# Two pairs of squared scores in one buffer, and one DMA transpose of 2048 columns in place of two of 1024

## The chip, the core and the metric

The kernel runs on one core of a Trainium2 chip. The metric is the device time of one execution in microseconds; lower is better. Shown for the kernel before are three runs: 765.41, 765.5 and 766.83 us, median 765.5 us. A profile is one further execution, taken by the hardware profiler. In it PE is TensorE (matmuls), PEld its loading of weights, DVE is VectorE, ACT is ScalarE, POOL is GpSimd, and SP is SyncE, whose queue issues nearly all DMAs of this kernel in program order.

## The reference

Two stages follow each other, for 8 batches of 3200 positions and 256 features.

```python
# first stage: z is 8 x 3200 x 64, u and v are 8 x 3200 x 256
scores = (1.0 / S) * np.matmul(z, z.transpose(0, 2, 1))
attn = np.maximum(scores, 0.0) ** 2
x = u * np.matmul(attn, v)
# second stage: w_q, w_k are 256 x 64, w_out is 256 x 256
W_tok = (1.0 / np.sqrt(dh)) * np.einsum('bsd,btd->bst', x @ w_q, x @ w_k)
mixed = np.einsum('bst,btd->bsd', W_tok, x)
out = np.maximum(mixed, 0.0) @ w_out
```

The score matrix of a batch is symmetric, since both of its factors are z. Only the first stage needs it element by element; in the second, `(x w_q)((x w_k)^T x)` is reassociated, so that a 64 x 256 matrix stands between.

## The kernel before

**Tiles of scores.** A batch's 3200 columns are split into seven groups: six of 512 columns and a last one of 128 (`LASTG`). The 3200 rows are 25 row tiles of 128. A *tile* in the list `tiles` (L253 to L281) is one row tile of scores for one group, 128 x 512; for the last group four row tiles of 128 columns make one. Tiles are handled in pairs: `scores(p0)` (L296) has TensorE fill two PSUM banks, one tile in each, `first_stage` (L316) has DVE or ACT take the positive part into an SBUF tile `g` (float32), and `second_stage` (L326) has ACT or POOL square `g` into an SBUF tile `at` of 2 x 512 columns in float16. `at` then serves as the stationary operand of the product with v (`second_product`, L464), which adds over all 25 row tiles into the accumulators `acc`.

**Turned tiles.** Since the scores are symmetric, a tile of group gi whose rows lie in a later group gj is, transposed, a tile of group gj. `is_turned(gi, gj)` (L237) says for which pairs of groups this is used: gj up to two further than gi, and (0, 4), never with the last group. That makes ten pairs of groups a batch, of four row tiles each. Their squares are turned by a DMA transpose from `at` into a tile `tt` (L342 to L352), one `tt` for each pair of groups, and when group gj is computed, the rows in question are not scored again but read from `tt`; these rows are the list `left` of the main loop (L1106). Row tile 24 of groups 3, 4 and 5 is turned likewise into small tiles `ts` for the last group. The seven `tt` buffers are planned at L285 to L293.

**Order of the tiles.** For each group the loop at L254 lists the turned row tiles (`near`) and the others (`own`) in twos, interleaved evenly, so that both tiles of a turned pair are neighbours and lie in one `at`; `odd` puts a tile ahead where a group starts at an odd place in the list. In `second_stage`, two neighbouring turned tiles become one transpose of 1024 columns (L340), a lone one a transpose of 512. The first group of the first batch has the order in which z arrives (`ZCH`).

**Buffers.** The pool `pat` hands out `NAT` = 11 buffers of one pair each, in turn (L50, L63). A buffer is filled again once TensorE has read all of it and its transposes have landed. The first four of them hold z, cast to float16, at the start (`zd`, L117 to L121), which TensorE turns at L130.

**The main loop.** One iteration (L1028 to L1231) scores up to three pairs (n = 6 tiles), takes the first stage of these, squares the pairs scored in the iteration before (`waiting`, L1080 to L1095), and has TensorE add up the tiles scored two iterations before (`LAG` = 2, L1099), a share of `left` with them (L1123). The order of instructions on every engine is that of the program, as written out by this loop and by the two scripts `OPENING` and `ENDING`. On SP's queue the transposes of `at` take their turn with those of x (L518), of the keys (L551) and of z (L176), with the loads of u (L195) and of v and z (L147), and with the stores of the output (L740). When a group closes, `gate` (L488) multiplies by u. Projections, keys, mixing and output of earlier groups are laid between the products.

**TensorE in two lanes.** Most matmuls contract over 64 of the 128 rows, and two of them run side by side in the two halves of the array (`first_pass`, `second_pass`, L401 to L418): each half of an `at` tile is read in one pass and the other half in the other.

```python
        ready = made_by[k - LAG]
...
        rows_ = [t for _, _, tis in tiles[consumed : consumed + new] for t in tis]
        old = len(left) if closes else min(len(left), max(0, size - len(rows_)))
        rows_ += left[:old]
        left = left[old:]
```

Of the kernel before, what the change touches and what calls it, by code (L numbers as in the profile page):

```python
# [9 lines left out]
FP16 = mybir.dt.float16  # L10
# [6 lines left out]
def kernel(  # L17
# [10 lines left out]
    nc = tc.nc  # L28

    B, S, D = u.shape  # L30
    dqk = z.shape[2]
    dh = moe_w_q.shape[1]
    P = 128
    NT = S // P
    ND = D // P
    W = 512
    widths = [512] * 6 + [128]
    starts = [sum(widths[:i]) for i in range(len(widths))]
# [8 lines left out]
    ALPHA = C1 * float(S) * float(S)  # L47
    FINAL_SCALE = 1.0 / (8.0 * ALPHA * ALPHA * ALPHA)

    NAT = 11  # L50

    consts = ctx.enter_context(tc.tile_pool(name="consts", bufs=1))
    pz = ctx.enter_context(tc.tile_pool(name="pz", bufs=1))
# [8 lines left out]
    pfo = ctx.enter_context(tc.tile_pool(name="pfo", bufs=2))  # L62
    pat = ctx.enter_context(tc.tile_pool(name="pat", bufs=NAT))  # L63
    ptt = ctx.enter_context(tc.tile_pool(name="ptt", bufs=1))
# [39 lines left out]
    zd0 = {}  # L104
# [12 lines left out]
    def cast_first(c, half, by):  # L117
        n0, nn = ZCH[c]
        if half == 0:
            zd0[c] = pat.tile([P, nn, 2, dqk], FP16, tag="at", name="zd")  # L120
        cast_by[by](out=zd0[c][:, :, half, :], in_=z32[n0][:])  # L121

    def turn_first(c):
# [111 lines left out]
    LASTG = NG - 1  # L235

    def is_turned(gi, gj):  # L237
        return gi < gj < LASTG and (gj <= gi + FAR or (gi, gj) == (0, 4))
# [5 lines left out]
    def group_of(ti):  # L244
        return max(gi for gi in range(NG) if starts[gi] <= ti * P)

    def rows_of(gi):
        return [starts[gi] // P + n for n in range(widths[gi] // P)]
# [4 lines left out]
    tiles, ends = [], {}  # L253
    for b in range(B):  # L254
        for gi in range(NG):
            near = [t for t in range(NT) if is_turned(gi, group_of(t))]
            own = [
                t for t in range(NT) if t not in near and not is_turned(group_of(t), gi)
            ]
            if gi == LASTG:  # L260
                own = [t for t in own if group_of(t) not in FOR_SMALL]
            if b == 0 and gi == 0:
                order = [t for n0, nn in ZCH for t in range(n0, n0 + nn)]
                assert sorted(order) == sorted(near + own)
            else:
                odd = len(tiles) % 2
                order, rest = own[:odd], own[odd:]
                n_, m_ = len(near) // 2, (len(rest) + 1) // 2
                at_ = sorted(
                    [((i + 0.5) / max(n_, 1), near[2 * i : 2 * i + 2]) for i in range(n_)]  # L270
                    + [((i + 0.7) / max(m_, 1), rest[2 * i : 2 * i + 2]) for i in range(m_)]
                )
                for _, two in at_:
                    order = order + two
                if rest and len(rest) % 2:
                    order.remove(rest[-1])
                    order.append(rest[-1])
            many = W // widths[gi]
            tiles += [(b, gi, order[i : i + many]) for i in range(0, len(order), many)]
            ends[b, gi] = len(tiles)  # L280
    NTILE = len(tiles)  # L281
# [4 lines left out]
    for b, gi, tis in tiles:  # L286
        gj = group_of(tis[0])
# [6 lines left out]
    made, turned = {}, {}  # L294
# [21 lines left out]
    def first_stage(p0, sc, on_act):  # L316
# [6 lines left out]
            )  # L323
        return g

    def second_stage(p0, g, on_act):  # L326
        at = pat.tile([P, 2 * W], FP16, tag="at", name="at")
        out = at[:].rearrange("p (a w) -> p a w", a=2)
        if on_act:
            nc.scalar.square(out=out, in_=g[:])  # L330
        else:
            nc.gpsimd.tensor_mul(out=out, in0=g[:], in1=g[:])  # L332
        blocks, turns = [], []
        for h, (b, gi, tis) in enumerate(tiles[p0 : p0 + 2]):
            for i, ti in enumerate(tis):
                made[b, gi, ti] = (at, h * W + i * widths[gi])
            gj = group_of(tis[0])
            if is_turned(gi, gj) or (gj == LASTG and gi in FOR_SMALL):
                blocks.append((b, gi, gj, tis[0] - starts[gj] // P, 1, h * W, (h + 1) * W))
        if len(blocks) == 2 and blocks[0][:3] == blocks[1][:3] and blocks[1][3] == blocks[0][3] + 1:  # L340
            blocks = [blocks[0][:4] + (2, blocks[0][5], blocks[1][6])]
        for b, gi, gj, n0, nn, c0, c1 in blocks:  # L342
            if gj == LASTG:
                turned[b, gi, gj] = ptt.tile([P, 1, 4, P], FP16, tag=f"ts{gi}", name=f"ts{gi}")
            elif (b, gi, gj) not in turned:
                home = tt_of[b, gi, gj]
                turned[b, gi, gj] = ptt.tile([P, 4, 4, P], FP16, tag=f"tt{home}", name=f"tt{home}")
            out = turned[b, gi, gj][:].rearrange("p n j t -> p (n j) t")
            turns.append(
                lambda out=out[:, 4 * n0 : 4 * (n0 + nn), :], c0=c0, c1=c1:  # L350
                nc.sync.dma_start_transpose(out=out, in_=at[:, c0:c1])
            )  # L352
        return turns

    accs = {}

# [44 lines left out]
    def first_pass(streams, banks, across):  # L401
        ends_ = {}

        def emit(lane, i, rows):
            ends_[lane] = i.emit(rows, i.start, False)

        for lane, rows in enumerate((LOW, HIGH)):
            for i in banks[lane ^ across]:
                streams.add(lane, width(i), lambda lane=lane, i=i, rows=rows: emit(lane, i, rows))
        return banks, across, max(streams.at), ends_  # L410
# [481 lines left out]
    now = [0]  # L892
# [74 lines left out]
    def shares(begins, closes, split, n):  # L967
        key = "s" if split else "b" if begins else "c" if closes else "m"
        key += "x" if mixing else "k" if keying else "p" if projecting else ""
        return shares_of[key][:n]  # L970
# [18 lines left out]
    def opening(order):  # L989
        sc, g = {}, {}  # L990
        for word in order.split():
            what, n, by = word[0], int(word[1:2]), word[2:]
            if what == "z":
                cast_first(n, int(by[0]), by[1])
            elif what == "t":
                turn_first(n)
            elif what == "c":
                place_first(n, by)
            elif what == "v":
                load_first_v(*[(0, 4), (12, 6), (18, 7), (4, 8)][n])  # L1000
            elif what == "s":
                sc[n] = scores(2 * n)
            elif what == "e":
                g[n] = first_stage(2 * n, sc.pop(n), by == "A")
            elif what == "q":
                each(second_stage(2 * n, g.pop(n), by == "A"))
            elif what == "w":
                warm(2 * int(word[1:]))
            elif what == "u":
                load_u(0, 0)  # L1010
            elif what == "m":
                ti = [t for x in tiles[2 * n : 2 * n + 2] for t in x[2]]
                for fn in whole(second_product(0, 0, ti, n == 0, False)):
                    fn()
        return [(2 * n, g[n]) for n in sorted(g)]
# [9 lines left out]
    left, first_sizes = [], [4, 5, 5, 5]  # L1025
    gate_pending = False
    ahead = []
    while groups:  # L1028
# [3 lines left out]
        n = 6  # L1032
# [7 lines left out]
        if mix_due(k):  # L1040
# [3 lines left out]
            n = 4  # L1044
        n = min(n, NTILE - produced)
# [45 lines left out]
        for i, x in enumerate([x for x in seconds if not x[2]]):  # L1091
            (late if i else soon).extend(second_stage(*x))
        for x in acts[:1]:
            each(second_stage(*x))
# [5 lines left out]
        b, gi = groups[0]  # L1100
        if begins:
# [4 lines left out]
            left = [t for t in range(NT) if t not in scored]  # L1106
        need = ends[b, gi]
        rest = len(left) + sum(len(tis) for _, _, tis in tiles[consumed:need])
# [7 lines left out]
        closes = steps == 1  # L1116
# [4 lines left out]
                new -= 1  # L1121
        rows_ = [t for _, _, tis in tiles[consumed : consumed + new] for t in tis]
        old = len(left) if closes else min(len(left), max(0, size - len(rows_)))  # L1123
        rows_ += left[:old]
        left = left[old:]
        consumed += new
# [10 lines left out]
        if on_lanes:  # L1137
# [7 lines left out]
            at_ = shares(begins, closes, split, len(between_))  # L1145
# [5 lines left out]
            if split:  # L1151
                cut = len(rows_) // 4
                if extra:
                    first = first_pass(streams, extra[0], across)
# [5 lines left out]
            elif extra and begins and uneven(extra):  # L1160
                first_extra = first_pass(streams, extra[0], across)
                first = first_pass(streams, banks, across)
# [3 lines left out]
            elif extra and begins:  # L1166
                first = first_pass(streams, extra[0], across)
                marks = [max(streams.at)]
                extra_second(first)
                first = first_pass(streams, banks, across)  # L1170
# [5 lines left out]
                at_ = [(x - 1) / total for x in marks + marks[1:]][: len(between_)]  # L1176
            elif extra:
                n_ = max(2, min(len(banks[0]) - 2, len(banks[0]) // 2))
                first = first_pass(streams, [bank[:n_] for bank in banks], across)
                first_extra = first_pass(streams, extra[0], across)  # L1180
                first = (banks, across) + first_pass(streams, [bank[n_:] for bank in banks], across)[2:]
# [35 lines left out]
        if closes:  # L1217
# [7 lines left out]
            left = None  # L1225
# [128 lines left out]
```

## Time and profile before

| | |
|---|---|
| median of three runs | 765.5 us (765.41 to 766.83) |
| span of the profiled execution, first to last instruction | 763.7 us |
| mean granted TensorE clock in it | 0.998 |
| bytes moved by DMA | 150.23 MB, mean 197 GB/s |
| DMA packets | 289614, of which 265168 under 512 B |
| read from HBM, written to HBM | 59.38 MB, 26.21 MB |

The profiled execution's own time is not given apart from its span; what lies around the span is taken as the difference to the median. In the tables of the profile a row names the line of the kernel, the engine, the operation and the tiles (out<-in), then the count. Busy times of an engine are unions over its instructions; the durations of matmuls are modelled at their ends. Duration triples are minimum, median and maximum in ns. "Landing" of a DMA is the time from the start of its issue to its completion. In a table of waits each row has who waited, for whom, us in total, number of times, longest.

### The profile page before, as it was taken

The numbers are of one execution on the slowest core, as the hardware profiler recorded it, in microseconds if no ns is written. First come the engines' busy times: TensorE is split into PE (matmuls) and PEld (weight loads), VectorE is DVE, ScalarE is ACT, GpSimd is POOL, SyncE is SP. The second block draws the span as 40 slices with busy tenths as digits, with TensorE's granted clock in tenths as the row PEclk, the third lists the DMA queues.
The fourth block names the chain that finished last, engine by engine and source line by source line (L and its number), as shares of the span: only waits on it lengthen the run. The fifth ranks groups of instructions, "written<-read, shape, count | busy, mean of one in ns | idle before, by whom it ended". The sixth has DMA issues, their size and how long they took to land.

```text
span 763.7 us, 29059 instructions
## 1 busy us (share of the span) xinstructions
PE 754.3 (99%) x12888; PEld 618.0 (81%) x12888; DVE 461.9 (60%) x458; ACT 551.1 (72%) x651; POOL 537.1 (70%) x351
## 2 busy tenths in 40 slices
PE   9999999999999999999999999999999999999996
PEld 6777888888888887888888888888878888888884
DVE  7655676546755567555665557656566565755534
ACT  8666776677767777687776877759777697776555
POOL 7897797768766678676787668866688665854540
PEclk9999999999999999999999999999999999999999
DMA  8999789887999969997899998999899999798636
GB/s 178 189 197 219 187 187 192 174 181 160 206 196 233 219 166 185 221 235 195 214 177 219 243 195 181 158 228 265 135 223 189 228 250 156 161 222 193 176 74 262
DMA packets 289614, 150.23 MB, mean 197 GB/s; under 512 B 265168, under 2 KB 268752, under 8 KB 289488
## 3 DMA queue, kind: packets, MB, share of 16 engines
q1 hardware_dynamic: 288768, 146.48, 91.2%
q0 software_dynamic: 576, 1.64, 1.1%
q8 instruction: 100, 1.64, 0.9%
q14 instruction: 26, 0.21, 0.1%
q10 hardware_dynamic: 144, 0.26, 0.1%
HBM read 59.38 MB, written 26.21 MB: 112 GB/s over the span
## 4 chain that ended last, share of the span: by engine, by line
PE 97%; DVE 2%; issue 0%; DMA 0%; ACT 0%; DVEq 0%; ACTq 0%
PE acc L369 72%; PE sc L307 12%; PE fo L369 5%; PE qk L369 5%; PE mx L657 1%; DVE x_sb L507 1%; DVE fo L1312 0%; DVE g L321 0%; PE ztp L130 0%; DMA z<-in_z_dram 0%; PE qk L610 0%; DVE zT L136 0%; PE xtx L634 0%; PE hd L644 0%; ACT fo L1316 0%
## 5 line engine op out<-in xcount | busy, mean ns | idle before, releaser
L321 DVE TENSOR_SCALAR g<-sc 128x1024 f32<-128x1024 f32 x329 | 400.5, 1223 | 240.5 <-PE sc L307 225.9
L332 POOL TENSOR_TENSOR at<-g 128x1024 f16<-128x1024 f32 x229 | 431.4, 1893 | 131.1 <-DVE g L321 106.5
L369 PE MATMUL acc<-v_sb,at 64*128 64x256 f16 (+1 forms) x7187 | 461.8, 269 | 1.6 <-DVE x_sb L507 0.5
L369 PEld LDWEIGHTS <-at 64*128 64x128 f16 (+1 forms) x7187 | 353.9, 94 | 86.9 <-PE acc L369 25.4
L330 ACT ACTIVATE at<-g 128x1024 f16<-128x1024 f32 x227 | 236.1, 1056 | 14.3 <-DVE g L321 7.2
L369 PE MATMUL acc<-v_sb,tt 64*128 64x256 f16 x2552 | 178.7, 269 | 0.0
L307 PE MATMUL sc<-zT 64*128 64x512 f16 (+1 forms) x1008 | 165.3, 357 | 0.2
L319 ACT ACTIVATE g<-sc 128x1024 f32<-128x1024 f32 x127 | 130.0, 1024 | 45.5 <-PE sc L307 43.2
L369 PEld LDWEIGHTS <-tt 64*128 64x128 f16 x2552 | 130.1, 94 | 14.2
L509 POOL TENSOR_TENSOR x_sb<-gt,u_sb 128x512 f16<-128x512 f32 x48 | 61.2, 1276 | 66.2 <-ACT gt L506 61.8
L678 ACT ACTIVATE rt<-mx 128x1024 f16<-128x1024 f32 x47 | 47.9, 1024 | 32.6 <-PE mx L657 32.5
L506 ACT COPY gt<-acc 128x512 f32<-128x512 f32 x48 | 28.0, 584 | 46.5 <-PE acc L369 44.7
L307 PEld LDWEIGHTS <-zT 64*128 64x128 f16 x1008 | 51.9, 94 | 8.8 <-issue 1.7
L369 PE MATMUL fo<-wo,rt 64*128 64x256 f16 (+1 forms) x696 | 57.9, 270 | 0.0
L544 ACT CAST qk<-qk 128x512 f16<-128x512 f32 x47 | 27.5, 585 | 34.3 <-PE qk L369 31.6
L369 PEld LDWEIGHTS <-rt 64*128 64x128 f16 (+1 forms) x696 | 35.5, 94 | 15.3 <-PE fo L369 6.3
L507 DVE TENSOR_TENSOR x_sb<-acc,u_sb 128x512 f16<-128x512 f32 x48 | 33.2, 691 | 20.3 <-PE acc L369 19.5
L739 ACT ACTIVATE fo<-fo 128x1024 f32<-128x1024 f32 x39 | 39.9, 1024 | 1.9 <-PE fo L369 1.7
L369 PEld LDWEIGHTS <-x_sb 64*128 64x128 f16 x672 | 29.8, 95 | 4.5 <-PE qk L369 0.9
L369 PE MATMUL qk<-kx,x_sb 64*128 64x64 f16 x672 | 32.8, 190 | 0.0
L369 PE MATMUL qk<-xT_sb,wkq 64*128 64x512 f16 (+3 forms) x118 | 25.8, 326 | 0.0
L369 PE MATMUL qk<-xT_sb,wqk 64*128 64x384 f16 (+3 forms) x148 | 24.8, 296 | 0.0
(86 smaller groups left out, 275.2 us busy)
## 6 DMA issues: line engine op xcount, KB each, us to landing
u_sb<-in_u_dram SPq DMA_DIRECT2D x48, 512.0 KB, 5.5
out_dram<-fo SPq DMA_DIRECT2D x43, 512.0 KB, 4.1
piece<-in_v_dram SPq DMA_DIRECT2D x42, 512.0 KB, 5.2
piece<-in_z_dram SPq DMA_DIRECT2D x7, 512.0 KB, 5.2
tt<-at SPq DMA_TRANSPOSE x162, 4.6
out_dram<-fo SPq DMA_DIRECT2D x9, 256.0 KB, 2.9
piece<-in_z_dram SPq DMA_DIRECT2D x7, 288.0 KB, 4.9
u_sb<-in_u_dram SPq DMA_DIRECT2D x8, 128.0 KB, 4.2
```

Source lines behind the costliest of these rows:

```text
L307: nc.tensor.matmul(out=sc[:, h, at : at + w], lhsT=zT[b][half : half + dqk, ds(z_at(b, h) + ti * P, P)], rhs=zT[b][half : half + dqk, ds(z ...
L319: nc.scalar.activation(out=g[:], in_=sc[:], func=RELU, scale=GSCALE)
L321: nc.vector.tensor_scalar(out=g[:], in0=sc[:], scalar1=0.0, scalar2=GSCALE, op0=AOP.max, op1=AOP.mult)
L330: nc.scalar.square(out=out, in_=g[:])
L332: nc.gpsimd.tensor_mul(out=out, in0=g[:], in1=g[:])
L369: return nc.tensor.matmul(out=self.out, lhsT=self.lhsT(rows), rhs=self.rhs(rows), start=start, stop=stop)
L506: nc.scalar.copy(out=upper[:], in_=accs[1][:])
L507: nc.vector.tensor_mul(out=x[:, 0:n], in0=accs[0][:, 0:n], in1=ug[:, 0:n])
L509: nc.gpsimd.tensor_mul(out=x[:, n : 2 * n], in0=upper[:], in1=ug[:, n : 2 * n])
L544: nc.scalar.copy(out=qks[b, gi][:, 0:gw], in_=out)
L678: nc.scalar.activation(out=out, in_=ps[:], func=RELU)
L739: nc.scalar.mul(out=flat_out[:, sl], in_=part, mul=FINAL_SCALE)
```

## The change

Five edits go together.

1. `pat` has 5 buffers of 2048 columns in place of 11 of 1024. Two pairs that follow each other in `tiles` (a *double*, numbered p0 // 4) share one: the pair that is squared first takes the buffer, the other one fills the second half.
2. The chunks of z at the start share buffers in twos.
3. The list of tiles puts turned and other row tiles in fours, with the start of a four at a multiple of 4 in the list.
4. The transposes of a double are issued after its second square has been emitted, and neighbouring turned tiles of one pair of groups go in one transpose, up to 2048 columns. Row tile 24 for the last group is still turned by itself, and at once.
5. In `left`, rows whose transposes have all been issued are moved to the front before a share is taken.

```diff
-    NAT = 11
+    NAT = 5
...
         if half == 0:
-            zd0[c] = pat.tile([P, nn, 2, dqk], FP16, tag="at", name="zd")
+            if c % 2 == 0:
+                zd0["both"] = pat.tile([P, 2, 8, 2, dqk], FP16, tag="at", name="zd")
+            zd0[c] = zd0["both"][:, c % 2, 0:nn, :, :]
...
-                odd = len(tiles) % 2
+                odd = -len(tiles) % 4
                 order, rest = own[:odd], own[odd:]
-                n_, m_ = len(near) // 2, (len(rest) + 1) // 2
+                n_, m_ = len(near) // 4, (len(rest) + 3) // 4
                 at_ = sorted(
-                    [((i + 0.5) / max(n_, 1), near[2 * i : 2 * i + 2]) for i in range(n_)]
-                    + [((i + 0.7) / max(m_, 1), rest[2 * i : 2 * i + 2]) for i in range(m_)]
+                    [((i + 0.5) / max(n_, 1), near[4 * i : 4 * i + 4]) for i in range(n_)]
+                    + [((i + 0.7) / max(m_, 1), rest[4 * i : 4 * i + 4]) for i in range(m_)]
                 )
...
+    doubles = {}
+
     def second_stage(p0, g, on_act):
-        at = pat.tile([P, 2 * W], FP16, tag="at", name="at")
-        out = at[:].rearrange("p (a w) -> p a w", a=2)
+        first = p0 // 4 not in doubles
+        if first:
+            doubles[p0 // 4] = pat.tile([P, 4 * W], FP16, tag="at", name="at"), []
+        at, parts = doubles[p0 // 4]
+        here = 2 * W * (p0 // 2 % 2)
+        out = at[:, here : here + 2 * W].rearrange("p (a w) -> p a w", a=2)
...
+                n0, c0 = tis[0] - starts[gj] // P, here + h * W
+                parts.append([b, gi, gj, n0, 1, c0, c0 + W])
+        blocks, turns = [], []
+        if first and p0 // 4 < (NTILE - 1) // 4:
+            now_, parts[:] = [x for x in parts if x[2] == LASTG], [x for x in parts if x[2] != LASTG]
+            parts = now_
+        else:
+            parts.sort(key=lambda x: x[5])
+        for part in parts:
+            was = blocks[-1] if blocks else None
+            if was and was[:3] == part[:3] and was[3] + was[4] == part[3] and was[6] == part[5]:
+                was[4] += 1
+                was[6] = part[6]
+            else:
+                blocks.append(part)
...
+    def turn_blocks(out, in_, key, tis):
+        for ti in tis:
+            turned_by[key + (ti,)] = now[0]
+        nc.sync.dma_start_transpose(out=out, in_=in_)
...
         old = len(left) if closes else min(len(left), max(0, size - len(rows_)))
+        if not closes:
+            left.sort(key=lambda t: not all((b, group_of(t), n) in turned_by for n in rows_of(gi)))
         rows_ += left[:old]
```

More of the change, by code (lines that the diff above doesn't have):

```diff
@@ L265 @@
             else:
-                odd = len(tiles) % 2
+                odd = -len(tiles) % 4
                 order, rest = own[:odd], own[odd:]
-                n_, m_ = len(near) // 2, (len(rest) + 1) // 2
+                n_, m_ = len(near) // 4, (len(rest) + 3) // 4
                 at_ = sorted(
-                    [((i + 0.5) / max(n_, 1), near[2 * i : 2 * i + 2]) for i in range(n_)]
-                    + [((i + 0.7) / max(m_, 1), rest[2 * i : 2 * i + 2]) for i in range(m_)]
-                )
[L273 to L277, printed above, removed]
+                    [((i + 0.5) / max(n_, 1), near[4 * i : 4 * i + 4]) for i in range(n_)]
+                    + [((i + 0.7) / max(m_, 1), rest[4 * i : 4 * i + 4]) for i in range(m_)]
+                )
+                for _, four in at_:
+                    order = order + four
+                short = rest[len(rest) // 4 * 4 :]
+                for t in short:
+                    order.remove(t)
+                order += short
             many = W // widths[gi]
@@ L332, in second_stage @@
             nc.gpsimd.tensor_mul(out=out, in0=g[:], in1=g[:])
-        blocks, turns = [], []
         for h, (b, gi, tis) in enumerate(tiles[p0 : p0 + 2]):
             for i, ti in enumerate(tis):
-                made[b, gi, ti] = (at, h * W + i * widths[gi])
+                made[b, gi, ti] = (at, here + h * W + i * widths[gi])
             gj = group_of(tis[0])
             if is_turned(gi, gj) or (gj == LASTG and gi in FOR_SMALL):
-                blocks.append((b, gi, gj, tis[0] - starts[gj] // P, 1, h * W, (h + 1) * W))
-        if len(blocks) == 2 and blocks[0][:3] == blocks[1][:3] and blocks[1][3] == blocks[0][3] + 1:
-            blocks = [blocks[0][:4] + (2, blocks[0][5], blocks[1][6])]
+                n0, c0 = tis[0] - starts[gj] // P, here + h * W
[13 more added lines that the diff above has]
+                blocks.append(part)
         for b, gi, gj, n0, nn, c0, c1 in blocks:
@@ L348, in second_stage @@
             out = turned[b, gi, gj][:].rearrange("p n j t -> p (n j) t")
+            tis = [starts[gj] // P + n0 + n for n in range(nn)]
             turns.append(
-                lambda out=out[:, 4 * n0 : 4 * (n0 + nn), :], c0=c0, c1=c1:
-                nc.sync.dma_start_transpose(out=out, in_=at[:, c0:c1])
-            )
-        return turns
+                lambda out=out[:, 4 * n0 : 4 * (n0 + nn), :], c0=c0, c1=c1, key=(b, gi), tis=tis:
+                turn_blocks(out, at[:, c0:c1], key, tis)
+            )
+        return turns
+    turned_by = {}
+    def turn_blocks(out, in_, key, tis):
+        for ti in tis:
+            turned_by[key + (ti,)] = now[0]
+        nc.sync.dma_start_transpose(out=out, in_=in_)
     accs = {}
```

## The prediction

> **What bounds the kernel now.** I read the page first, then the table by stretches, then the views of the tile `at`, then the DMA queue.
>
> ```profile
> span 763.7 us, 29059 instructions
> PE 754.3 (99%) x12888; PEld 618.0 (81%) x12888; DVE 461.9 (60%) x458; ACT 551.1 (72%) x651; POOL 537.1 (70%) x351
> PE 97%; DVE 2%; issue 0%; DMA 0%; ACT 0%; DVEq 0%; ACTq 0%
> ```
>
> TensorE works nearly all the time, and the chain that ended last is 97% TensorE with no share for DMA. The other compute engines have 28 to 40% to spare. Where the rest lies, the stretches show (columns after the length: busy time of PE, PEld, DVE, ACT, POOL, with instruction counts; then granted clock, DMA share, GB/s):
>
> ```profile
> 0.00:15.00 15.00, 13.77 (x129) 9.37 (x131) 9.35 (x14) 11.83 (x13) 9.28 (x16) 1.00 0.81 173
> 15.00:30.00 15.00, 14.73 (x239) 11.47 (x236) 11.83 (x12) 11.59 (x13) 15.00 (x9) 1.00 0.83 160
> 30.00:100.00 70.00, 69.73 (x1192) 56.27 (x1190) 40.60 (x39) 49.28 (x58) 56.89 (x50) 1.00 0.99 198
> ...
> 700.00:740.00 40.00, 40.00 (x654) 32.96 (x650) 19.05 (x19) 24.48 (x28) 19.46 (x11) 1.00 0.59 151
> 740.00:763.70 23.70, 17.07 (x139) 12.45 (x137) 9.69 (x14) 10.93 (x17) 1.27 (x1) 0.95 0.62 222
> ```
> ```profile
> 15.00:740.00 725.00, 723.43 (x12627) 596.19 (x12623) 442.85 (x432) 528.36 (x621) 526.52 (x335) 1.00 0.95 196
> ```
>
> Between 15 and 740 us TensorE is idle for 725.00 - 723.43 = 1.57 us in all, at full clock. The idle 6.6 us of the tail lie after the last `at` tile is read; they belong to scaling and storing the output, which the change leaves alone. So hardly anything can be won here, and anything that makes TensorE wait is paid in full. What TensorE itself waited for by the waits view:
>
> ```profile
> PE sc L981 <- DVE zeros L1018: 1.0, 1, 1.0
> PE acc L369 <- DVE x_sb L507: 0.5, 3, 0.2
> ```
>
> No DMA and no square of scores stands there. "Busy" is modelled and can hide short stalls, so 1.57 us is a guide to the possible gain, not a wall.
>
> **The part that changes: squares, buffers, turns.**
>
> ```profile
> L332 POOL TENSOR_TENSOR at<-g x229: 1882/1892/1907, 10.2 to 733.9; 128x1024 f16<-128x1024 f32 x115
> L330 ACT ACTIVATE at<-g x227: 1040/1057/1080, 6.3 to 735.7; 128x1024 f16<-128x1024 f32 x114
> L351 SPq DMA_TRANSPOSE tt<-at x162: 1195/1373/4432, 13.1 to 719.6; - x162
> L351 SPq DMA_TRANSPOSE ts<-at x24: 1194/1253/2101, 62.7 to 736.3; - x24
> ```
>
> 229 + 227 = 456 squares start in 735.7 - 6.3 = 729.4 us, one each 1.60 us. The code scores three pairs an iteration, so an iteration is 4.8 us; LAG = 2 has the pairs scored in one iteration squared in the next and read by TensorE in the one after.
>
> **Term 1, turns on the SyncE queue.** Per batch ten combinations (gi, gj) are turned, four tiles each. Two to a turn that is 20 x 8 = 160, plus 2 in the first group, where tile 24 shifts the pairs: the 162 of the row. Four to a turn I worked out from the new order: 78 of four, 2 of three, 2 single ones, 82 in all, so 80 issues go. The 24 `ts` turns stay. What a turn of 2048 columns costs the queue no row shows. The nearest, by columns: 256 (`xTl`), 512 (`ts` above), 1024 (`xT_sb`, and `tt` above):
>
> ```profile
> L518 SPq DMA_TRANSPOSE xT_sb<-x_sb x48: 1232/1249/2976, 34.3 to 742.5; - x48
> L518 SPq DMA_TRANSPOSE xTl<-xl x8: 1168/1172/1827, 98.2 to 744.5; - x8
> ```
>
> 1.17, 1.25, 1.25 to 1.37 us: nearly flat. I take 1.4 us, with twice `tt`, 2.75 us, as upper end. At 1.4 the queue gets back about 80 x 1.37 = 110 us over the run; at 2.75 nothing. In neither case does the end move at once: nothing on TensorE waits for that queue. The SyncE queue matters only through when buffers come free (term 2).
> The Trainium skill, *DMA: Bandwidth & Descriptors*, in its table of sequencer times under "Why a DMA increments its semaphore by 16 and not by 1", puts generations before the newest at 262,144 cycles for a turn of 8,192 small tiles, one push a tile. By that a turn of twice the columns issues for twice as long, which is the upper end and speaks against the change; the near-flat rows here disagree as far as 1024 columns, and none goes further.
>
> **Term 2, the buffers.** Eleven buffers of one pair become five of two pairs: SBUF for ten pairs, handed out in twos. A buffer was refilled 11 x 1.60 = 17.6 us after its previous fill; now 5 x 2 x 1.60 = 16.0 us. And it is held longer: until both pairs are read, and where it is turned, until a turn has landed that can only be issued when the second square is done. How late the queue is for a square that is done, a stretch of the fifth batch shows:
>
> ```profile
> 404.82 1.89 POOL L332 TENSOR_TENSOR at<-g 128x1024 f16<-128x1024 f32 x1 [1.36 <-DVE g L321]
> ```
> ```profile
> 410.92 1.35 SPq L351 DMA_TRANSPOSE tt<-at  x1
> 412.37 1.36 SPq L551 DMA_TRANSPOSE kx<-qk  x1
> 413.83 4.12 SPq L351 DMA_TRANSPOSE tt<-at  x2
> 418.00 1.44 SPq L147 DMA_DIRECT2D piece<-in_v_dram  x1
> 419.55 1.24 SPq L518 DMA_TRANSPOSE xT_sb<-x_sb  x1
> 420.89 1.80 SPq L351 DMA_TRANSPOSE tt<-at  x1
> ```
>
> The square of rows 16 and 17 of the fourth group ends at 404.82 + 1.89 = 406.71 and its turn is the first of the two at 413.83, 7.1 us later; the queue is never free in between, and of the 11.8 us shown 7.3 go to `tt` turns. From queue free to queue full the wait w is thus 0 to 7.1 us. Landing, median from issue, by size:
>
> ```profile
> tt<-at SPq DMA_TRANSPOSE x162, 4.6
> ts<-at SPq DMA_TRANSPOSE x24, 4.3
> xTl<-xl SPq DMA_TRANSPOSE x8, 2.6
> ```
>
> 512 to 1024 columns adds 0.3; 256 to 1024 adds 2.0, or 0.67 for each 256, which makes 2.7 for 1024 more. So 2048 columns land in 4.9 to 7.3 us, at most 9.2 (twice); I take the middle, 6.1. A turned buffer is then held for 1.6 (the second pair) + 1.9 (its square) + w + 6.1 = 9.6 + w, that is 9.6 to 16.7 against 16.0. One double in three straddles two iterations and can be held 3.2 us more (4.8 in place of 1.6): 12.8 + w, up to 19.9. With the queue's `tt` work halved I take w as halved, 0 to 3.5: even a straddler is then late by 0.3 us at most.
> What a late buffer costs: it stops ACT or POOL before the square, with the later evictions, gate copies and output scalings behind it. It happens already:
>
> ```profile
> ACT at L330 <- DMA tt<-at: 3.2, 1, 3.2
> ```
>
> That wait fell between 20 and 45 us, and TensorE's whole idle time from 30 to 100 us is 70.00 - 69.73 = 0.27 us. So a wait of 3 us is about covered, which fits the code: a square is due one iteration ahead of its reader, 4.8 - 1.9 = 2.9 us to spare. For the whole run the bounds are: nothing, if no double is late; and with w unrelieved, 27 straddlers of 81 turned doubles, late when w > 3.2 (55%, 15 of them, 2.0 us each) = 29 us of waiting, priced at 0.27/3.2 us of TensorE each, 2.4 us. I take +0.3 us, near the lower end, since halved w leaves almost none late.
>
> **Term 3, what the old wait gives back.** In the new order the doubles of the second group come as 7,16,17,18 / 8 to 11 / 19 to 22, so the buffer that ACT waited for there is one that is only read, not turned. At most 0.27 us come back, at least none (the same wait elsewhere); I take -0.2.
>
> **Small edits, at nothing.** The first casts (`zd`) fill two doubles in place of four of the eleven:
>
> ```profile
> L130 PE MATMUL ztp<-ident,zd x25: 216/219/314, 3.4 to 10.5; 128*128 128x128 f16 x25
> ```
>
> They are read by 10.5 us, and the first square that needs one again is the seventh, not before 6.3 + 6 x 1.06 = 12.7 us even if ACT ran them all without a pause. Lost, that cover costs one square, 1.1 to 1.9 us. The order of scores and the sort of the leftover rows change no count of matmuls. The turns of (4, 5), nearest to their reader, now end with the eighth or tenth of that group's 13 tiles, before with the twelfth: two to four tiles, 1.6 to 3.2 us, earlier.
> The Trainium skill's *DMA: Bandwidth & Descriptors*, "Rules for kernel authors", says to coalesce small transfers because they are mostly overhead. By it the turns get cheaper, which term 1 grants; it would move the time only where something waits for them.
>
> **Sum.** 763.7 of the profiled span, 765.5 - 763.7 = 1.8 between it and the median of the runs, 0 + 0.3 - 0.2: 765.6 us. A measurement of this kernel tells about 0.2%, 1.5 us, from no change.
>
> **Rivals.**
> *Slower: a late double starves the squares.* For it: the queue is packed, buffers shrink by one pair, and TensorE has no slack. If 2048 columns cost the queue twice and land in 7.3 us, w stays 0 to 7.1 and a straddler is held 14.0 + w. It is late by w - 2.0, beyond the 2.9 of cover from w = 4.9 on: 31% of 27, 8 doubles, at a mean of 1.1, 9 us: 774.5. With a little relief, w up to 6.1, it is 20% of 27, 5 doubles at 0.6, 3 us: 768.5; with 9.2 us of landing and none, 16 doubles at 2.05, 33 us: 798. Against it: the flat issue rows. Chance 0.26.
> *Faster: short stalls hidden in TensorE's busy time go with the freed queue.* All 1.57 us gone: 763.9; below that only what the model of matmul ends hides. For it: the wait on `tt` early on. Against it: no TensorE wait names a DMA. Chance 0.17.
> *It does not relieve the queue, but the buffers bear it:* issue 2.75, landing 6.1, with half of the 2.4 us of term 2's upper bound: 765.5 + 1.2 = 766.7. Chance 0.15, half on either side of 0.2%.
> *Forecast:* 0.42.
>
> Same: 0.42 + 0.08 = 0.50; slower 0.26 + 0.07 = 0.33; faster 0.17. The range 763.8 to 770.0 leaves out a third of the faster rival and half of the slower one, about 0.2. The likeliest case alone is 765.0 to 766.5.
>
> **What would show it.** Right: 82 `tt` turns with issue near 1.4 and landing near 6 us, ACT and POOL waiting less than 10 us in all for `tt` landings, TensorE idle between 15 and 740 us under 2.5 us. Wrong: issue near 2.8, waits of `at` on `tt` in tens of us, and TensorE waiting for L330 or L332; or a busy time of TensorE that falls although its instructions stay.

## The result, and the profile after

The changed kernel takes 769.32 us (median of seven runs, 768.52 to 774.6), the kernel before 765.5 us (seven runs, 765.18 to 766.83): a ratio of 1.0066, 95% interval 1.0043 to 1.0089 (it is not the ratio of the two medians, which is 1.0050). It is slower, by 3.8 us between the medians, and it also scatters more: 6.1 us from lowest to highest, before 1.7. The profiled execution is the 768.52 of these, the fastest, so its loss of 3.0 us is less than that of the median.

The page and the table by stretches of the changed kernel, in the columns shown before:

```profile
span 766.7 us, 28922 instructions
PE 753.5 (98%) x12888; PEld 617.6 (81%) x12888; DVE 462.0 (60%) x458; ACT 551.4 (72%) x651; POOL 537.2 (70%) x351
PE 92%; DMA 2%; DVE 2%; POOL 2%; issue 1%; ACT 1%; POOLq 0%; ACTq 0%; DVEq 0%
```
```profile
0.00:15.00 15.00, 12.60 (x127) 9.19 (x129) 9.27 (x13) 11.82 (x13) 9.46 (x16) 1.00 0.86 200
...
100.00:200.00 100.00, 99.40 (x1744) 81.76 (x1742) 60.98 (x61) 70.81 (x84) 77.73 (x48) 1.00 0.90 188
...
600.00:700.00 100.00, 97.86 (x1726) 80.95 (x1722) 60.80 (x61) 74.78 (x90) 63.67 (x41) 1.00 0.89 189
```
```profile
15.00:740.00 725.00, 721.12 (x12604) 593.54 (x12601) 441.92 (x430) 528.10 (x621) 526.43 (x335) 1.00 0.93 195
```

No engine has more to do than before. TensorE is idle for 3.88 us between 15 and 740 us, before 1.57, and 2.14 of it lie between 600 and 700 us alone. The chain, 97% TensorE before, now has DMA, POOL and ACT on it. (In the first 15 us TensorE is busy for 1.17 us less than before. That is no work of the change: the experiment with the old opening and the new order of tiles shows 12.90 there, and the one that leaves out the sort but has the new opening 13.69, so this stretch varies by about a microsecond from one execution to the next, whichever opening it has.)

The rows of the tile `at`, and the waits of its two writers, in the changed kernel:

```profile
L341 POOL TENSOR_TENSOR at<-g x229: 1885/1893/1910, 10.0 to 736.6; 128x1024 f16<-128x1024 f32 x115
L339 ACT ACTIVATE at<-g x227: 1039/1057/1097, 6.1 to 738.5; 128x1024 f16<-128x1024 f32 x114
L381 SPq DMA_TRANSPOSE tt<-at x82: 1322/3426/6322, 14.2 to 717.2; - x82
L381 SPq DMA_TRANSPOSE ts<-at x24: 1194/1230/2282, 65.1 to 739.0; - x24
```
```profile
ACT at L339 <- DMA tt<-at: 20.9, 11, 4.1
...
POOL at L341 <- DMA tt<-at: 18.7, 9, 3.4
```
```profile
tt<-at SPq DMA_TRANSPOSE x82, 6.2
```

There are 82 turns in place of 162, and they land 6.2 us after their issue. But the issue of one takes 3.43 us at the median, not 1.37: the queue got nothing back. And squares now wait 20.9 + 18.7 = 39.6 us in all for a turn to land, before 4.8 us.

How such a wait reaches TensorE, the stretch around 663 us shows. First the SyncE queue, then ACT, then who waited from 660 to 668 us:

```profile
653.93 8.23 SPq L381 DMA_TRANSPOSE tt<-at  x2
```
```profile
657.81 1.05 ACT L339 ACTIVATE at<-g 128x1024 f16<-128x1024 f32 x1
662.91 1.06 ACT L339 ACTIVATE at<-g 128x1024 f16<-128x1024 f32 x1 [4.06 <-DMA tt<-at]
663.88 1.01 ACT L322 ACTIVATE g<-sc 128x1024 f32<-128x1024 f32 x1
664.78 0.58 ACT L572 CAST qk<-qk 128x512 f16<-128x512 f32 x1
```
```profile
ACT at L339 <- DMA tt<-at: 4.1, 1, 4.1
...
PE sc L310 <- ACT g L322: 1.8, 1, 1.8
```

ACT stands for 4.06 us before a square whose buffer is still being turned for its last double: that turn is the first of the two in the SyncE row, and it lands at 662.8. Behind the square in ACT's program is an eviction of scores (L322) that TensorE needs: its PSUM banks come free only at 664.9, and TensorE, with no free banks for its next scores, stands for 1.8 us. Here it is ACT's order of work that passes the wait on, not the late square itself. This one gap holds 1.8 of the 2.3 us that TensorE lost between 15 and 740 us. In that stretch TensorE has one other gap of over 0.25 us, 0.33 us at 116 us, before a product that waits for a square itself; the kernel before has none.

### The profile page after: what moved, and what is told of

Read it like the earlier page. It is cut to its first block, busy times and chain, and to the rows that moved or that the text cites. A ratio compares the mean times of both kernels' runs of the same rounds, so it can differ in the third digit from the quotient of the medians.

```text
span 766.7 us, 28922 instructions
## 1 busy us (share of the span) xinstructions
PE 753.5 (98%) x12888; PEld 617.6 (81%) x12888; DVE 462.0 (60%) x458; ACT 551.4 (72%) x651; POOL 537.2 (70%) x351
## 4 chain that ended last, share of the span: by engine, by line
PE 92%; DMA 2%; DVE 2%; POOL 2%; issue 1%; ACT 1%; POOLq 0%; ACTq 0%; DVEq 0%
PE acc L397 69%; PE sc L310 12%; PE fo L397 5%; PE qk L397 4%; PE mx L685 1%; POOL at L341 1%; DMA tt<-at 1%; DMA v_sb<-in_v_dram 1%; DVE x_sb L535 1%; DVE g L324 0%; DVE fo L1342 0%; PE qk L638 0%; DVE zT L138 0%; POOL x_sb L537 0%; PE xtx L662 0%
## 5 line engine op out<-in xcount | busy, mean ns | idle before, releaser
L341 POOL TENSOR_TENSOR at<-g 128x1024 f16<-128x1024 f32 x229 | 431.2, 1894 | 135.6 <-DVE g L324 90.4
L339 ACT ACTIVATE at<-g 128x1024 f16<-128x1024 f32 x227 | 236.2, 1055 | 31.0 <-DMA tt<-at 20.9
L322 ACT ACTIVATE g<-sc 128x1024 f32<-128x1024 f32 x127 | 130.0, 1024 | 36.2 <-PE sc L310 34.2
L706 ACT ACTIVATE rt<-mx 128x1024 f16<-128x1024 f32 x47 | 47.9, 1024 | 32.0 <-PE mx L685 31.8
```

The lines of the kernel that those rows point to most:

```text
L322: nc.scalar.activation(out=g[:], in_=sc[:], func=RELU, scale=GSCALE)
L706: nc.scalar.activation(out=out, in_=ps[:], func=RELU)
```

## The experiments

The question was which of the change's parts makes the buffers late: the order of the tiles, the wide turn, the turn that waits for the second square, or two pairs sharing one buffer of five. All times are medians; *idle* is TensorE's idle time between 15 and 740 us and *waits* the time that squares waited for a turn to land (`tt` and `ts` together), both in one profiled execution.

| kernel | buffers x pairs | turn | waits, us | idle, us | time, us | ratio (95%) |
|---|---|---|---|---|---|---|
| before | 11 x 1 | 1024 | 4.8 | 1.57 | 765.5 | |
| changed | 5 x 2 | 2048 | 39.6 | 3.88 | 769.32 | 1.0066 (1.0043 to 1.0089) |
| e1_split | 5 x 2 | 2 x 1024 | 89.1 | 6.82 | 771.44 | 1.0097 (1.0068 to 1.0125) |
| e2_own | 5 x 2 | 1024, each pair at once | 52.1 | 5.40 | 769.74 | 1.0051 (1.0039 to 1.0063) |
| e3_order | 11 x 1 | 1024 | 8.0 | 1.67 | 765.34 | 1.0001 (0.9992 to 1.0009) |
| e5_six | 6 x 2 | 2048 | 7.2 | 1.72 | 765.33 | 1.0000 (0.9992 to 1.0009) |
| b12 | 12 x 1 | 1024 | 0 | 1.56 | 765.01 | 0.9998 (0.9989 to 1.0007) |
| b10 | 10 x 1 | 1024 | 21.1 | 1.57 | 765.48 | 1.0007 (0.9996 to 1.0019) |
| b9 | 9 x 1 | 1024 | 46.3 | 3.73 | 768.24 | 1.0034 (1.0022 to 1.0047) |
| e6_nosort | 5 x 2 | 2048 | 60.0 | 4.16 | 771.39 | 1.0076 (1.0063 to 1.0089) |
| e8_nostore | 5 x 2 | 2048 | 47.3 | 4.03 | 769.26 | 1.0042 (1.0029 to 1.0055) |
| e9_six_split | 6 x 2 | 2 x 1024 | 7.9 | 1.57 | 765.17 | 0.9996 (0.9987 to 1.0005) |
| e10_nou | 5 x 2 | 2048 | 0.8 | 1.57 | 765.82 | 1.0002 (0.9993 to 1.0011) |

**e1_split: turns of 1024, else as changed.**

```diff
-            if was and was[:3] == part[:3] and was[3] + was[4] == part[3] and was[6] == part[5]:
+            if was and was[4] < 2 and was[:3] == part[:3] and was[3] + was[4] == part[3] and was[6] == part[5]:
```

> The changed kernel, with each turn of 2048 columns issued as two of 1024 at the same place in the queue; order, sharing of buffers and the wait for the second square stay. Theory size (the 2048-column turn, 3.43 us of issue, keeps the queue full): issue of a turn back to 1.3 to 1.4 us, the squares' waits on tt, 39.6 us in the changed kernel, fall under 15 us, time under 767.0. Theory hold (a buffer of two pairs, refilled after 16 us, is held until the turn of its second pair has landed): the waits stay between 20 and 50 us and the time between 767.5 and 772.

What the squares waited for, and the turns, in the rows of `at`:

```profile
L381 SPq DMA_TRANSPOSE tt<-at x162: 1210/1454/4964, 12.8 to 721.5; - x162
...
  DMA tt<-at: 72.1, 31
...
  DMA ts<-at: 17.0, 8
```

The issue of a turn is back at 1.45 us, and the waits more than doubled, to 89.1 us, beyond what either theory named. Given five doubles, two narrow turns hold them longer than one wide one: from the first square to the landing a quarter of the turned doubles takes more than 16.6 us here, and more than 15.6 us in the changed kernel. So the loss does not go away with the wide turn, and the theory of size falls.

**e2_own: each pair turned at its own square, five doubles stay.**

```diff
-        if first and p0 // 4 < (NTILE - 1) // 4:
-            now_, parts[:] = [x for x in parts if x[2] == LASTG], [x for x in parts if x[2] != LASTG]
-            parts = now_
-        else:
-            parts.sort(key=lambda x: x[5])
+        parts, kept = list(parts), parts
+        kept[:] = []
```

> The changed kernel, with every pair turned at its own square, 1024 columns at most; order and sharing of five buffers stay. Theory hold, by way of the late turn: waits of squares on tt under 12 us, time 765.3 to 766.8. Theory capacity (five buffers of two pairs are too few, whenever the turn is issued): waits stay over 20 us, time 767.5 or more. Theory size alone gives the same as with two turns at the second square, within 0.5 us.

```profile
L378 SPq DMA_TRANSPOSE tt<-at x162: 1197/1386/4276, 13.4 to 720.2; - x162
...
  DMA tt<-at: 46.3, 24
...
  DMA ts<-at: 5.8, 2
```

Waits of 52.1 us and 769.74 us: the turn that waits for the second square is not the cause either. It is not free, though: the same narrow turns at the second square, in e1_split, waited 89.1 us and took 1.7 us longer. What e1, e2 and the changed kernel have in common is five buffers of two pairs.

**e3_order: the new order of tiles in the kernel before.** Only the block from `odd = ...` to `order += short` of the change is put in.

> The kernel before with the new order of the tiles alone (fours, aligned to four); eleven buffers, turns of 1024. Theories hold, capacity and size: as before, 765.0 to 766.3, waits of squares on tt under 8 us. Theory order (four turned tiles in a row crowd the queue): waits over 15 us and 767 or more.

```profile
ACT at L331 <- DMA tt<-at: 5.8, 3, 4.6
```

765.34 us, waits 8.0 us, at the edge of what was expected and without a clear effect on TensorE (idle 1.67 us), although one of the waits lasted 4.6 us. Fours in a row cost nothing that can be measured.

**e5_six: six doubles.**

```diff
-    NAT = 5
+    NAT = 6
...
-    px = ctx.enter_context(tc.tile_pool(name="px", bufs=7))
+    px = ctx.enter_context(tc.tile_pool(name="px", bufs=6))
```

> The changed kernel with six buffers of two pairs (refilled after 19.2 us, not 16.0), paid for with one of the seven buffers of x. Theories hold and capacity: waits of squares on tt under 5 us, TensorE idle between 15 and 740 us near 1.6, time 765.0 to 766.3, unless the lost buffer of x costs. Theory size or order: TensorE still loses 2 us or more, time 767.5 or more.

```profile
L381 SPq DMA_TRANSPOSE tt<-at x82: 1317/3328/6350, 14.0 to 714.6; - x82
...
  DMA tt<-at: 6.6, 5
...
  DMA ts<-at: 0.6, 1
```
```profile
15.00:740.00 725.00, 723.28 (x12625) 595.71 (x12620) 442.74 (x431) 528.60 (x621) 526.87 (x335) 1.00 0.94 196
```

765.33 us. The turns are as wide and as slow to issue as in the changed kernel (3.33 us), and with one more double the whole loss is gone. The buffers are the place of the loss, and the buffer of x that paid for it does not show as missed. The waits, at 7.2 us, are a little over the 5 us expected. The change as it stands wins nothing even so: it equals the kernel before.

**b10, b9, b12: single buffers, ten, nine and twelve.** `NAT` alone in the kernel before; for twelve also one buffer of x less, as in e5_six.

> The kernel before with ten single buffers, the SBUF that five doubles take; refilled after 16.0 us as in the changed kernel, but each pair freed by itself. Theory doubles (what costs is that two pairs are freed together, by the later of them): waits of squares on tt 8 to 20 us, at 0.08 us of TensorE for each (3.2 us over 39.6 us of waits in the changed kernel) 765.5 to 767.0. Theory bytes (the SBUF for ten pairs in place of eleven is what costs): as the changed kernel, waits 35 us or more, 768.5 or more.

> The kernel before with nine single buffers, refilled after 14.4 us. Theory doubles: five doubles act like nine to ten singles, since the first pair of a double waits for both pairs of five doubles ago, nine and ten pairs back; so waits of 25 to 60 us and 767.5 to 770.5, near the changed kernel. Theory bytes: far slower than the changed kernel, 773 or more.

> The kernel before with twelve single buffers, paid for with one of the seven buffers of x. If the waits of squares (4.8 us before) still cost TensorE, they go to under 2 us and the time to 764.9 to 765.2; the rival has nothing left to win: 765.2 to 765.6.

The waits in the rows of `at`, for ten buffers (with the longest of them) and for nine, and TensorE from 15 to 740 us in the same two:

```profile
  DMA tt<-at: 20.2, 12
...
  DMA ts<-at: 0.9, 1
```
```profile
POOL at L332 <- DMA tt<-at: 12.0, 7, 3.5
```
```profile
  DMA tt<-at: 46.3, 26
```
```profile
15.00:740.00 725.00, 723.43 (x12626) 596.11 (x12622) 442.69 (x431) 528.31 (x621) 526.14 (x335) 1.00 0.96 196
```
```profile
15.00:740.00 725.00, 721.27 (x12602) 594.23 (x12597) 441.66 (x430) 528.38 (x620) 525.94 (x335) 1.00 0.96 196
```

Ten singles take as much SBUF as five doubles and cost nothing that can be measured; nine cost 2.9 us, close to the changed kernel's 3.8, with waits (46.3 us) like its own. So it is not the bytes: a double is handed out only when both its pairs are free, so its first pair waits for a pair nine back, and by this count five doubles act like nine singles, and six like eleven, which fits e5_six. (The count leaves out when the turn is issued, so it can't tell e1_split from e2_own.) b10 shows something else: 21.1 us of waits, a little over the 8 to 20 expected, the longest of 3.5 us, left TensorE's idle time at 1.57 us. These waits were covered. The 3.2 us of TensorE that its expectation divides by 39.6 are 2.3 by the tables above. (One of its eleven runs took 770.18 us, so ten is at the edge.) Twelve singles take all waits away; 765.01 us lies where the first theory put it, but the interval (0.9989 to 1.0007) holds no change as well, and TensorE's idle time is the 1.56 us of before, which speaks for the rival, whose range it misses by 0.2 us.

**e6_nosort: the changed kernel without the sort of `left`.**

> The changed kernel without the sort of the leftover rows. Theory capacity: the sort has no part in it, 768 to 771, waits 30 to 55 us. Rival (rows read earlier or later by the sort move the end of the reads): under 767 or over 772.

771.39 us and waits of 60.0 us, both a little above what the first theory named and on neither side that the rival named, with an interval that overlaps the changed kernel's. The sort is not the cause; it may help, which these runs do not settle.

**e8_nostore and e10_nou: what keeps the doubles.** Both leave out work: the first the main loop's stores of the output, the second also all loads of u but one.

```diff
-            queue.dma_start(
+            if not groups: queue.dma_start(
...
-        us[b, gi] = pu.tile([P, 4, D], FP32, tag="u_sb", name="u_sb")
-        nc.sync.dma_start(out=us[b, gi][:, 0:nn, :], in_=rows(u, b)[:, n0 : n0 + nn, :])
+        if "one" not in us:
+            us["one"] = pu.tile([P, 4, D], FP32, tag="u_sb", name="u_sb")
+            nc.sync.dma_start(out=us["one"][:, 0:nn, :], in_=rows(u, b)[:, n0 : n0 + nn, :])
+        us[b, gi] = us["one"]
```

> The changed kernel without the stores of the output that go out in the main loop (leaves out 38 or so stores of 512 KB, so most of the output stays unwritten); five doubles and turns of 2048 stay. Theory: the doubles are late because their turns share the queue and the DMA engines with everything else; with some 20 of 150 MB gone, the waits of squares on tt fall under 20 us (39.6 with the stores) and the time under 767. Rival (the doubles are late by the schedule of squares and reads alone, whatever the DMAs do): waits stay over 30 us, 768 or more.

> The changed kernel without the main loop's stores of the output and with u loaded once only (leaves out 55 loads of u and some 38 stores, a third of the bytes that DMAs move). If what is left of the lateness is crowding by other DMAs: waits of squares on tt under 25 us (47.3 without the stores alone) and the time under 767. If it is the turns themselves and the schedule of squares: waits still over 35 us, 768 or more.

Without the stores, the rows of `at` have:

```profile
L381 SPq DMA_TRANSPOSE tt<-at x82: 1322/3483/5435, 14.2 to 717.9; - x82
...
  DMA tt<-at: 47.3, 22
```

That is no better than with them, 769.26 us: it is what the rival named, and against the theory of crowding as I had put it. Without the loads of u too, the same rows and the bytes on the DMA engines:

```profile
L383 SPq DMA_TRANSPOSE tt<-at x82: 1317/2984/5011, 13.8 to 714.1; - x82
...
  DMA tt<-at: 0.8, 1
```
```profile
DMA packets 273515, 104.05 MB, mean 136 GB/s; under 512 B 261104, under 2 KB 263664, under 8 KB 273392
```

The waits all but vanish (0.8 us), against the rival, and 765.82 us equals the kernel before: five doubles with wide turns are enough once the other DMAs are thinned out. I matched every turned buffer with its squares and its turn in program order. From the last square of a buffer to the issue of its turn passed, at the median, 4.98 us in the kernel before, 4.11 in the changed one, 3.48 without stores and 1.25 without u as well. From the first square to the landing it was 11.1 us before, for single pairs, and 13.5, 12.9 and 10.6 for doubles; a quarter of the changed kernel's turned doubles exceeded 15.6 us. The buffer is due again after 16.0 us only on average: counted from first square to first square, with the waits for turns taken off, one buffer in four was due within 14.0 us and one in twenty within 11.5. In the changed kernel the queue was issuing other DMAs for 290 of the 324 us that finished doubles waited for their turn's issue. So it is crowding, but taking out the stores alone does not relieve it. Whether the loads of u crowd by their issues or by the DMA engines' time, and what it does to leave them out with the stores in place, these runs leave open.

**e9_six_split: narrow turns with six doubles.** e1_split and e5_six in one.

> Six doubles, with turns of two times 1024 columns at the second square. If the size of a turn matters only through late buffers, six doubles hide it: 765.0 to 766.3, as with turns of 2048 (765.33). If the wide turn is worth something by itself (fewer issues): 766.5 or more.

765.17 us, waits 7.9 us. With enough buffers the width of a turn is worth nothing that can be measured, in either direction.

## Why the prediction was wrong

*What bounds the kernel*: right. The loss is TensorE's waiting, and spare buffers beyond enough gained nothing that can be measured (b12, e9_six_split).

*Term 1, the queue*: the count of turns (82) was right; the price was the step that failed. "I take 1.4 us, with twice `tt`, 2.75 us, as upper end": a turn of 2048 columns is issued in 3.43 us at the median, above that end. Over all DMAs of the queue the issues add up to 614.5 us before (503 of them) and 623.2 after (423), so the 110 us of relief were not there. The rows up to 1024 columns are flat at the median, and I carried on a flat line by another factor of two.
The median hides what the price goes with. I sorted the turns by how many of the queue's earlier DMAs had not landed when the issue began. In the changed kernel the median issue is 1.83 us with one of them in flight (11 turns), 3.09 with two (28), 4.34 with three (28) and 5.26 with four (12). The kernel before showed the same, more weakly: 1.29, 1.32, 1.38 and 1.92 us for turns of 1024 columns, and 2.17 with five. So the wide turns were cheap only where little was in flight, and in this kernel two or more mostly are. What the issue waits for there, these runs do not show.
The Trainium skill's rule that I weighed there (*DMA: Bandwidth & Descriptors*, "Why a DMA increments its semaphore by 16 and not by 1", one push a small tile) has the issue double with the columns; the page puts it for "previous generations" and does not name this chip. The median here went up even more, and the shortest of the 82 turns, 1.32 us, does not fit it. The Trainium skill's rule on coalescing that the prediction also names (same page, "Rules for kernel authors") speaks of overhead under 64 KB. A turn of 1024 columns already moves 128 x 1024 x 2 B = 256 KB, so cheaper turns did not follow from it.

*Term 2, the buffers*: the landing time (6.1 us, measured 6.2) was right, and the worst-case hold near (19.9 us, measured up to 21.4). But "with the queue's `tt` work halved I take w as halved, 0 to 3.5" rested on term 1, and fell with it: the median wait for the issue went from 5.0 to 4.1 us, not to half, and its largest was 10.2 us. (The upper end of 7.1 us, read from one stretch, was too low too: the kernel before has up to 11.7.) So the +0.3 us should have been 2.3 in the profiled execution (3.88 - 1.57) and more in others. No run makes the wide turn itself cheap. But e10_nou, which empties the queue in another way, brings the median wait to 1.25 us and the loss to nothing that can be measured, which supports the step from w to the buffers. My bound for unrelieved w, 29 us of waiting, was below the measured 39.6 as well: I let only straddling doubles be late, with 4.8 us between their pairs. Squares waited for 15 doubles, and in 14 of them the two squares began at most 2.8 us apart. The period of 16.0 us was a mean as well: seven of the 15 had been held for less. The double of the case at 663 us had been held for 14.4 us and was due after 10.5.
The price, 0.27/3.2 us of TensorE for a microsecond of waiting, is near on average (0.08 against 2.3/39.6 = 0.06), but it is no constant: 21.1 us of waits in b10 cost nothing, 89.1 us in e1_split cost 6.82 - 1.57 = 5.25. Nor is the cover of 2.9 us a constant: 4.06 us on ACT cost TensorE 1.8 us in the case shown, more than the 1.2 beyond the cover, and 4.6 us on ACT in e3_order cost it 0.1 at most. What a wait costs seems to depend on what stands behind it in the engine's program; that was not tested.

*Term 3*: wrong, and small. In the changed kernel ACT waits between 20 and 45 us just as long, 3.3 us in two waits:

```profile
ACT at L339 <- DMA tt<-at: 3.3, 2, 2.9
```

*Small edits at nothing*: the order holds (e3_order). The opening shows no loss beyond its own scatter. Whether the sort gains anything stays open.

*Rivals*: what happened is the slower rival, a late double that starves the squares. It had a chance of 0.26 and the forecast 0.42. That its form "with a little relief" gives 768.5 us, near the measured 769.3, is luck: it counted five straddling doubles and 7.3 us of landing. The range to 770.0 held the median, but the forecast was no change, and the kernel is slower. Of the signs named for "wrong", issue over 2.8 us and waits in tens of us came true. TensorE waits for L322 (1.8 us) far more than for L339 (0.3), and not for L341.

## What to carry to other kernels

Merging buffers in twos at the same size in bytes takes away buffers: here five doubles cost about what nine singles cost, not ten, and a pool that has just enough singles will not do. Where a bound engine has no slack, ask before such a merge how long a buffer is held against how soon it is due, with the slowest quarter of the holds and the soonest quarter of the refills in place of the medians. Fewer DMA issues relieve a queue only if the wider one is not longer to issue in proportion; measure one on the queue as full as it will be before counting on it.

## What the runs showed of the hardware that was not expected

At the median, the issue of a DMA transpose on SyncE's queue takes 1.17 to 1.37 us from 256 to 1024 columns in the kernel before, and 3.43 us for 2048 in the changed one (2.98 with a third of all bytes gone, 1.32 at the least), so one wide issue can hold the queue longer than two narrow ones. The issue of the wide one goes with what is still in flight: 1.83 us with one earlier DMA of the queue not yet landed, 5.26 with four. The changed kernel's scatter from run to run (6.1 us, before 1.7) is smaller with six doubles: e5_six and e9_six_split lie within 764.85 and 767.36 us in 22 runs. Late buffers alone do not explain it, since b9 and e8_nostore, with waits as long, lie within 1.8 and 1.4 us in five runs each.
